# Queries times the per-head matrices: per pair with a block-diagonal matrix, or per head in 64-row tiles

## The chip, the cores and the metric

One NeuronCore of a Trainium2 chip runs the whole program in one launch. The metric is the device time of that launch in microseconds (us); lower is better. TensorE does matmuls (PE in the profile, its weight loads PEld), VectorE is DVE, ScalarE is ACT, SyncE (SP) issues the DMAs. PSUM, where matmuls write, has eight banks of 512 fp32 columns on 128 partitions.

## What is computed

Linear attention with a normalisation feeds two gated feed-forward layers one after the other.

```python
# q, k, v: (8 batches, 8 heads, 576 positions, 64)
kv  = einsum('bhsd,bhse->bhde', k, v)        # one 64x64 matrix per head
o   = einsum('bhsd,bhde->bhse', q, kv)       # the step that is changed
rms = sqrt(mean(o * o, axis=-1) + 1e-6)
x   = (o / rms * g_norm)  -> (4608 tokens, 512)
h   = x @ w_in;  x = (h * clip(h + 3, 0, 6) / 6) @ w_out    # layer 1, d_ff 2048
h   = x @ w_in2; y = (h * cos(h)) @ w_out2                  # layer 2, d_ff 2048
```

All inputs are fp32; the weights are held as float64 and decoded on the chip.

## The kernel before, in words

The 4608 tokens are 36 chunks of 128 tokens (`chunk`, L426) and nine token blocks of 512. A batch has 576 positions, so every ninth chunk from chunk 4 on (4, 13, 22, 31) lies across two batches; `parts` (L409) then gives two halves of 64 tokens. Heads go in four pairs (NP = 4).

`kv_pair` (L393) makes the two 64x64 matrices of a head pair in fp32: head 0 is written to PSUM partitions 0 to 63, head 1 to 64 to 127, and each is copied to its diagonal block of `kvbd` (L406), whose other blocks are zero. `chunk` then does, for 128 tokens: four transposes of q into the bank `pq` (L429), ACT's copy of it to `qT` (L440, head 0 of a pair on partitions 0 to 63, head 1 on 64 to 127), a pause of one turn (W1), the products `po` of the four pairs (L449), ACT's Square and Copy of `po` into `sq` and `ot` (L453, L454), the row sums and the reciprocal root (L459 to L467), the scaling (L469), a pause (W2), four transposes into `px` (L475) and ACT's copy into the layer's input (L481). In fp32 one matmul of the program is two weight loads and two matmul records in the trace; a transpose is one of each.

PSUM has eight one-bank buffers: `acc0` to `acc3`, `P`, `R` and two with the tag `t`. `ps_scratch` (L143) gives the attention its banks. In the prologue (chunks 0 to 3) it goes round the list of L871; after L963 every `kv`, `pq`, `po`, `px` and the tiny `pt` and `pb` of the scale computations take one of the two `t` banks, and so does the bank `Q` of each group of the first layer (L822). A third user waits until one of the two is read out.

The steps are generators that yield between operations; `turn` (L126) advances all that are active. `group` (L813) is one step of a layer's first product: seven products of fp16 operands (L835), after each of which two turns and some of the second product's matmuls (`mm2`, L654) are issued. `attention` (L977) starts a kv pair or a chunk every 0.44 groups, with at most two chunks under way. This gives the order of priority. A scheduler writes each engine's instruction list from it ahead of the launch; an instruction whose operands or bank aren't ready by its own reckoning is put behind ready ones. On the chip each engine runs its list in order.

From 0 to about 33 us the prologue runs, to 167 us the first token block in plain fp32 (L1012, L1027), to 687 us the first layer with the attention's other chunks beside it, and then the rest of both layers.

Of the kernel before, what the change touches and what calls it, by code (L numbers as in the profile page):

```python
# [12 lines left out]
AF = mybir.ActivationFunctionType  # L13
# [42 lines left out]
def attention_moe_kernel(  # L56
# [12 lines left out]
    nc = tc.nc  # L69
    B, H, S, D = q.shape  # L70
# [4 lines left out]
    P = 128  # L75
    NP = H // 2
# [38 lines left out]
    kvbd = const.tile([P, 2, NP, P], F32, name="kvbd")  # L115
# [27 lines left out]
    def ps_scratch(name):  # L143
        tag = scratch[turn_of[0] % len(scratch)]
        turn_of[0] += 1
        return ps_m.tile([P, 512], F32, tag=tag, name=name, bufs=2 if tag == "t" else 1)
# [262 lines left out]
    def parts(c):  # L409

        r, res = 0, []
        while r < P:
            b, s = divmod(c * P + r, S)
            n = min(P - r, S - s)
            res.append((b, s, r, n))
            r += n
        return res
# [8 lines left out]
    def chunk(c, qt, dst, after=None, tmp=None):  # L426
        pt = ps_scratch(f"pq{c}")
        for p in range(NP):
            nc.tensor.transpose(  # L429
                out=pt[:, p * P:(p + 1) * P],  # L430
                in_=qt[:, 2 * p:2 * p + 2, :].rearrange("p h d -> p (h d)"), identity=ident,
            )
        if tmp is not None:
            qT, ot, sq = (tmp[:, n] for n in range(3))
            ot, sq = (t.rearrange("p (h d) -> p h d", h=H) for t in (ot, sq))
        else:
            qT = at_p.tile([P, 512], F32, tag="qT", name=f"qT{c}")
            ot = at_p.tile([P, H, D], F32, tag="ot", name=f"ot{c}")
            sq = at_p.tile([P, H, D], F32, tag="sq", name=f"sq{c}")
        nc.scalar.activation(out=qT, in_=pt, func=AF.Copy)  # L440
        if after is not None:
            after()
        yield
        for _ in range(W1):
            yield
        po = ps_scratch(f"po{c}")
        for p in range(NP):
            for b, s, r, n in parts(c):
                nc.tensor.matmul(  # L449
                    out=po[r:r + n, p * P:(p + 1) * P], lhsT=qT[:, p * P + r:p * P + r + n],  # L450
                    rhs=kvbd[:, b % 2, p], start=True, stop=True,
                )
        nc.scalar.activation(out=sq, in_=po.rearrange("p (h d) -> p h d", h=H), func=AF.Square)  # L453
        nc.scalar.activation(out=ot, in_=po.rearrange("p (h d) -> p h d", h=H), func=AF.Copy)  # L454
        yield
        ss = sm_p.tile([P, H], F32, tag="ss", name=f"ss{c}")
        y = sm_p.tile([P, H], F32, tag="y", name=f"y{c}")
        t = sm_p.tile([P, H], F32, tag="t", name=f"t{c}")
        nc.vector.tensor_reduce(out=ss, in_=sq, axis=AX.X, op=ALU.add)  # L459
        nc.vector.tensor_scalar(out=ss, in0=ss, scalar1=1.0 / D, scalar2=1e-6, op0=ALU.mult, op1=ALU.add)  # L460
        yield
        nc.scalar.activation(out=y, in_=ss, func=AF.Abs_reciprocal_sqrt)
        yield
        nc.vector.tensor_tensor(out=t, in0=ss, in1=y, op=ALU.mult)
        nc.vector.tensor_tensor(out=t, in0=t, in1=y, op=ALU.mult)
        nc.vector.tensor_scalar(out=t, in0=t, scalar1=-0.5, scalar2=1.5, op0=ALU.mult, op1=ALU.add)
        nc.vector.tensor_tensor(out=y, in0=y, in1=t, op=ALU.mult)  # L467
        yield
        nc.vector.tensor_tensor(out=sq, in0=ot, in1=y[:, :, None].to_broadcast([P, H, D]), op=ALU.mult)  # L469
        yield  # L470
        for _ in range(W2):
            yield
        px = ps_scratch(f"px{c}")
        for p in range(NP):
            nc.tensor.transpose(  # L475
                out=px[:, p * P:(p + 1) * P],
                in_=sq[:, 2 * p:2 * p + 2, :].rearrange("p h d -> p (h d)"), identity=ident,
            )
        yield
        for kk, d in dst:  # L480
            nc.scalar.activation(  # L481
                out=d, in_=px[:, kk * P:(kk + d.shape[1]) * P].rearrange("p (k t) -> p k t", t=P),
                func=AF.Copy, scale=gs,
            )
        yield
# [458 lines left out]
    for p in range(NP):  # L944
        run(kv_pair(0, p, kv_t.pop((0, p)), tail))
    run(g_scale())
    isx = tiny("isx", scale["g"][1], imm=8.0)
    pro = [
        chunk(
            c, q_t.pop(c), [(2 * n, xr0[n][:, :, c * P:(c + 1) * P]) for n in range(2)],  # L950
            tmp=wi_p.tile([P, 3, 512], F32, tag="wi", name=f"tmp{c}") if c < 2 else None,
# [3 lines left out]
    n = 0  # L955
# [11 lines left out]
    def run_chunk(c, xr, after):  # L967
        j, n = divmod(c, 4)
        yield from chunk(c, q_t.pop(c), [(0, xr[:, :, n * P:(n + 1) * P])], after)
        free["at"] += 1  # L970
        x_done[j] = x_done.get(j, 0) + 1
        if x_done[j] == 4:
            xraw[0, j] = xr
# [121 lines left out]
    n = NG * (NSB - 2)  # L1095
# [36 lines left out]
```

## Time and profile before

| what | value |
|---|---|
| time, median of 3 runs | 1551.84 us (1547.57 to 1552.95) |
| time of the profiled execution | 1551.0 us |
| its span, first to last instruction | 1549.1 us |
| PE busy | 1516.1 us, 98% |
| DVE busy | 1226.3 us, 79% |
| ACT busy | 1052.3 us, 68% |
| mean granted TensorE clock | 0.998 |

The busy share is an average over stages. Whether an engine sets the time is read from each stage by itself, and from the chain of waits, which follows the work back from its end. A matmul's record lasts longer than the step from one to the next, because matmuls overlap in the array; what a burst costs is read from the distance of the starts.

### The profile page before, as it was taken

To read this page: it belongs to the slowest core of one execution; us is meant where nothing else is said; L and a number is where in the kernel's file an instruction comes from. 1 tells how busy PE (TensorE), PEld (TensorE's weight loads), DVE (VectorE), ACT (ScalarE), POOL (GpSimd) and SP (SyncE) were. 2 spreads that over 40 slices of the span, in tenths; PEclk is the share of its full clock that TensorE was granted. 3 is DMA by queue.
4 is the path that set the end of the run, shared out by engine and by line. 5 is a ranking of instruction groups with operands and counts; after the bars stand their busy time and mean duration, and the time that the engine had idled before them with its cause. 6 is when DMAs were issued, how large, how long until landed. Compare 5 with 4: busy or idle time off the path is not lost.

```text
span 1549.1 us, 28806 instructions
## 1 busy us (share of the span) xinstructions
PE 1516.1 (98%) x11902; PEld 1153.8 (74%) x11902; DVE 1226.3 (79%) x2234; ACT 1052.3 (68%) x1714; POOL 2.0 (0%) x8
## 2 busy tenths in 40 slices
PE   6999999999999999999999999999999999999998
PEld 6444676666667676766666678888888888888887
DVE  4899877786877687876475799989898989889881
ACT  4567665665666565665455788888888887878771
POOL 0000000000000000000000000000000000000000
PEclk9999999999999999999999999999999999999999
DMA  7653433325243342402031233343342424333434
GB/s 205 202 165 95 123 102 110 103 81 165 69 150 98 88 129 74 150 25 79 1 103 48 96 110 117 129 142 116 139 142 105 157 91 155 117 132 123 147 111 155
DMA packets 112067, 180.12 MB, mean 116 GB/s; under 512 B 51008, under 2 KB 83776, under 8 KB 102720
## 3 DMA queue, kind: packets, MB, share of 16 engines
q1 hardware_dynamic: 111936, 178.28, 34.9%
q8 instruction: 93, 1.52, 0.4%
q14 instruction: 38, 0.31, 0.1%
HBM read 144.70 MB, written 33.55 MB: 115 GB/s over the span
## 4 chain that ended last, share of the span: by engine, by line
PE 51%; DVE 31%; ACT 12%; DMA 3%; issue 2%; SPq 1%; ACTq 0%
PE acc L654 18%; PE P L835 10%; DVE uA L587 5%; PE R L835 5%; DVE uA L592 4%; DVE gs_A L264 4%; DVE gs_S L264 4%; ACT uA L589 3%; PE h L1012 3%; PE Q L835 3%; PE acc L1027 3%; DVE c L851 2%; ACT uA L590 2%; PE po L449 2%; PE P L707 2%
## 5 line engine op out<-in xcount | busy, mean ns | idle before, releaser
L835 PEld LDWEIGHTS <-wi 128*128 128x128 f16 x5712 | 557.3, 98 | 108.7 <-issue 5.1
L654 PE MATMUL acc<-g,wo 128*128 128x512 f16 x1536 | 368.9, 379 | 0.4 <-ACT g L561 0.3
L654 PEld LDWEIGHTS <-wo 128*128 128x128 f16 x1536 | 148.8, 98 | 135.0 <-issue 1.7
L835 PE MATMUL P<-xoB,wi 128*128 128x256 f16 x1536 | 190.3, 273 | 1.6 <-ACT sn L847 1.5
L835 PE MATMUL P<-xoT,wi 128*128 128x256 f16 x1536 | 189.1, 273 | 0.5 <-ACT sn L847 0.2
L707 PEld LDWEIGHTS <-gs_A 128*128 128x128 f16 x1632 | 159.7, 98 | 20.4 <-issue 1.9
L847 ACT ACTIVATE sn<-P 128x512 f32<-128x512 f32 x204 | 119.2, 584 | 63.3 <-PE P L835 62.7
L707 PEld LDWEIGHTS <-gs_S 128*128 128x128 f16 x1392 | 136.1, 98 | 22.0 <-issue 6.2
L589 ACT ACTIVATE uA<-uA,cols 128x512 f32<-128x512 f32 x144 | 103.6, 720 | 62.3 <-DVE uA L587 60.9
L548 ACT ACTIVATE u<-c,cols 128x512 f32<-128x512 f32 x96 | 77.9, 812 | 82.2 <-DVE c L851 62.3
L707 PE MATMUL P<-wo,gs_S 128*128 128x256 f16 x888 | 114.6, 273 | 5.0 <-ACT kv_buf L726 5.0
L563 DVE TENSOR_TENSOR g<-u,g 128x512 f16<-128x512 f32 x128 | 87.5, 687 | 30.1 <-ACT g L561 29.1
L707 PE MATMUL P<-wo,gs_A 128*128 128x256 f16 x840 | 107.2, 273 | 1.6 <-ACT kv_buf L726 1.6
L561 ACT ACTIVATE g<-u 128x512 f16<-128x512 f32 x128 | 80.1, 628 | 37.5 <-DVE u L550 36.9
L550 DVE SCALAR_TENSOR_TENSOR u<-u,cols,c 128x512 f32<-128x512 f32 x96 | 71.9, 749 | 39.7 <-ACT u L548 39.4
L262 ACT ACTIVATE gs_A<-uA,cols 128x512 f16<-128x512 f32 x125 | 88.3, 713 | 16.2 <-DVE uA L592 11.3
L264 DVE SCALAR_TENSOR_TENSOR gs_A<-uA,cols,gs_A 128x512 f16<-128x512 f32 x125 | 92.6, 746 | 7.1 <-ACT gs_A L262 5.1
L585 ACT ACTIVATE uA<-c,cols 128x512 int32<-128x512 f32 x108 | 77.2, 715 | 30.0 <-DVE c L856 21.8
L835 PE MATMUL R<-xoT,wi 128*128 128x256 f16 x768 | 94.7, 273 | 0.0
L835 PE MATMUL Q<-xoB,wi 128*128 128x256 f16 x768 | 94.6, 273 | 0.0
L835 PE MATMUL R<-xoN,wi 128*128 128x256 f16 x768 | 94.5, 273 | 0.0
L592 DVE SCALAR_TENSOR_TENSOR uA<-uA,c 128x512 f32<-128x512 f32 x108 | 74.1, 686 | 23.0 <-ACT uA L590 22.1
(205 smaller groups left out, 2242.4 us busy)
## 6 DMA issues: line engine op xcount, KB each, us to landing
wo<-wod SPq DMA_DIRECT2D x63, 1024.0 KB, 4.9
ri<-in_moe_w_in_dram SPq DMA_DIRECT2D x16, 1024.0 KB, 6.5
ro<-in_moe_w_out_dram SPq DMA_DIRECT2D x16, 1024.0 KB, 5.1
x2d<-o SPq DMA_DIRECT2D x36, 256.0 KB, 2.5
xr<-x2d SPq DMA_DIRECT2D x9, 1024.0 KB, 4.8
out_dram<-o SPq DMA_DIRECT2D x36, 256.0 KB, 4.0
q<-in_q_dram SPq DMA_DIRECT2D x30, 256.0 KB, 2.9
kv_buf<-in_k_dram SPq DMA_DIRECT2D x29, 256.0 KB, 2.9
```

The source lines that it names most:

```text
L262: nc.scalar.activation(out=hi, in_=src, func=AF.Copy, scale=s)
L264: nc.vector.scalar_tensor_tensor(out=lo, in0=src, scalar=s, in1=hi, op0=ALU.mult, op1=ALU.subtract)
L548: nc.scalar.activation(out=u, in_=c, func=AF.Relu, scale=u0[:, gi:gi + 1], bias=b0[:, gi:gi + 1])
L561: nc.scalar.activation(out=gt[:, :, 0, sl], in_=u, func=AF.Copy)
L563: nc.vector.tensor_tensor(out=gt[:, :, 1, sl], in0=u, in1=gt[:, :, 0, sl], op=ALU.subtract)
L587: stt(out=u, in0=ui, scalar=nk, in1=c, op0=ALU.mult, op1=ALU.add)
L589: nc.scalar.activation(out=u, in_=u, func=AF.Sin, scale=hf)
L592: stt(out=u, in0=u, scalar=0.5 * SIG2, in1=c, op0=ALU.subtract, op1=ALU.mult)
L654: nc.tensor.matmul(out=acc[e], lhsT=w[:, a, row, e * P:(e + 1) * P], rhs=g[:, c], start=(n == 0 and i == 0), stop=(n == NF - 1 and i == 2),)
L707: nc.tensor.matmul(out=ps[:, mt], lhsT=g[:, c, pr, mt * P:(mt + 1) * P], rhs=w[:, i, a], start=(first and k == 0), stop=(end and k == 2), ...
L835: nc.tensor.matmul(out=ps[bank][:, pr], lhsT=w[:, a, A_AT[an], kk], rhs=x[:, c, kk], start=(first and pr == 0 and i == 0 and kk == 0), sto ...
L847: nc.scalar.activation(out=sn[n], in_=ps["P"], func=AF.Copy)
```

## The change

The product of the queries with `kvbd` is made for each head by itself: contraction over the 64 partitions of that head (`hr`), 128 tokens (or 64) as weights, and the head's 64x64 block as the moving operand. The even heads of the four pairs go into one bank, the odd heads into another. ACT reads each bank with a Square and a Copy of 256 columns, written to every second head's place of `sq` and `ot`.

```diff
-        po = ps_scratch(f"po{c}")
+        po = [ps_scratch(f"po{h}_{c}")[:, 0:NP * D] for h in range(2)]
         for p in range(NP):
             for b, s, r, n in parts(c):
-                nc.tensor.matmul(
-                    out=po[r:r + n, p * P:(p + 1) * P], lhsT=qT[:, p * P + r:p * P + r + n],
-                    rhs=kvbd[:, b % 2, p], start=True, stop=True,
-                )
-        nc.scalar.activation(out=sq, in_=po.rearrange("p (h d) -> p h d", h=H), func=AF.Square)
-        nc.scalar.activation(out=ot, in_=po.rearrange("p (h d) -> p h d", h=H), func=AF.Copy)
+                for h in range(2):
+                    hr = slice(64 * h, 64 * h + 64)
+                    nc.tensor.matmul(
+                        out=po[h][r:r + n, p * D:(p + 1) * D], lhsT=qT[hr, p * P + r:p * P + r + n],
+                        rhs=kvbd[hr, b % 2, p, hr], start=True, stop=True,
+                    )
+        for h in range(2):
+            src = po[h].rearrange("p (m d) -> p m d", m=NP)
+            nc.scalar.activation(out=sq.rearrange("p (m o) d -> p m o d", o=2)[:, :, h], in_=src, func=AF.Square)
+            nc.scalar.activation(out=ot.rearrange("p (m o) d -> p m o d", o=2)[:, :, h], in_=src, func=AF.Copy)
```

## Rows read from the trace of the kernel before

**Rows 1.** The page: its span and the engines' busy time, share, instructions.
```profile
span 1549.1 us, 28806 instructions
PE 1516.1 (98%) x11902; PEld 1153.8 (74%) x11902; DVE 1226.3 (79%) x2234; ACT 1052.3 (68%) x1714; POOL 2.0 (0%) x8
```

**Rows 2.** Stretches: length, busy us of each engine, granted clock, DMA.
```profile
33.00:167.00 134.00, 131.56 (x515) 67.05 (x514) 115.12 (x240) 86.27 (x129) 0.00 (x0) 0.99 0.49 153
167.00:687.00 520.00, 514.45 (x3934) 357.29 (x3932) 397.18 (x831) 319.71 (x533) 0.00 (x0) 1.00 0.34 105
```

**Rows 3.** The chain of waits, 200 to 240 us: start, length, engine, tile, line.
```profile
209.57 0.89 PE po L449 x8
210.47 1.31 PE R L835 x12
211.78 0.44 PE px L475 x4
```

**Rows 4.** Line L449: duration ns min/median/max, first and last start, forms.
```profile
L449 PE MATMUL po<-kvbd,qT x304: 272/275/377, 20.7 to 670.7; 128*128 128x128 f32 x120, 128*64 128x128 f32 x32
```

**Rows 5.** Timeline at one-row matmuls: start, length, engine, line, operation, shapes, count.
```profile
411.11 0.29 PEld L160 LDWEIGHTS pb_o<-cols,ones_row 1*128 1x128 f32 x2 [0.66 <-DVE cols L155]
```

**Rows 6.** Line L160: its loads.
```profile
L160 PEld LDWEIGHTS pb_o<-cols,ones_row x16: 181/182/184, 57.2 to 685.2; 1*128 1x128 f32 x16
```

**Rows 7.** Timeline around one kv pair, 234.5 to 236.4 us.
```profile
234.68 0.60 PE L835 MATMUL R<-xoT,wi 128*128 128x256 f16 x4
...
235.20 0.66 PEld L401 LDWEIGHTS kv<-kv_buf 128*64 128x64 f32 x20 [0.21 <-issue]
235.21 0.80 PE L401 MATMUL kv<-kv_buf 128*64 128x64 f32 x20
...
235.94 0.82 PE L654 MATMUL acc<-g,wo 128*128 128x512 f16 x3
```

**Rows 8.** Line L401: its loads and matmuls.
```profile
L401 PEld LDWEIGHTS kv<-kv_buf x576: 132/138/232, 4.4 to 611.8; 128*64 128x64 f32 x192
L401 PE MATMUL kv<-kv_buf x576: 222/222/366, 4.4 to 611.9; 128*64 128x64 f32 x192
```

**Rows 9.** Timeline of chunk 13, whose tokens lie in two batches.
```profile
280.35 1.09 PE L449 MATMUL po<-kvbd,qT 128*64 128x128 f32 x16
...
281.38 0.39 PE L835 MATMUL R<-xoT,wi 128*128 128x256 f16 x2
```

**Rows 10.** Timeline, 220.6 to 224.2 us: another chunk's px just ahead of po.
```profile
221.38 1.06 PE L449 MATMUL po<-kvbd,qT 128*128 128x128 f32 x8
...
221.59 0.69 ACT L481 ACTIVATE x<-px,cols 128x512 f32<-128x512 f32 x1 [1.12 <-PE px L475]
...
223.35 0.59 ACT L454 ACTIVATE ot<-po 128x512 f32<-128x512 f32 x1
```

**Rows 11.** Timeline, 301.5 to 305.5 us: the same with ACT busy.
```profile
302.26 1.06 PE L449 MATMUL po<-kvbd,qT 128*128 128x128 f32 x8
...
303.60 0.67 ACT L481 ACTIVATE x<-px,cols 128x512 f32<-128x512 f32 x1
```

**Rows 12.** Timeline, 668.5 to 672.5 us: the last such place.
```profile
669.88 1.06 PE L449 MATMUL po<-kvbd,qT 128*128 128x128 f32 x8
```

**Rows 13.** Timeline of PE in the prologue, 14.5 to 21 us.
```profile
14.95 2.34 PE L449 MATMUL po<-kvbd,tmp 128*128 128x128 f32 x12
17.30 0.27 PE L153 MATMUL pt_g<-ident,cols 128*1 128x128 f32 x1
17.41 0.61 PE L449 MATMUL po<-kvbd,tmp 128*128 128x128 f32 x4
```

**Rows 14.** Lines L453 and L481 on ACT: 512 columns, and 256.
```profile
L453 ACT ACTIVATE sq<-po x34: 577/588/613, 22.4 to 671.3; 128x512 f32<-128x512 f32 x34
L481 ACT ACTIVATE x<-px,cols x32: 668/677/702, 107.5 to 681.9; 128x512 f32<-128x512 f32 x32
L481 ACT ACTIVATE xr<-px,cols x8: 463/470/475, 26.9 to 31.9; 128x256 f32<-128x256 f32 x8
```

## The prediction, made before the changed kernel was run

> **What bounds the kernel now.** I read the busy shares of the page first, then the stretches, then the chain of waits where the changed lines run, and last the timeline around them. The page gives PE 1516.1 of 1549.1 us [rows 1]; the stretches show that this is no average over idle and full parts: PE is busy for 131.6 of 134 us while the first token block runs and for 514.5 of 520 us while the other chunks of the attention do [rows 2]. In the second stretch ACT is busy for 319.7 us and DVE for 397.2. The chain of waits there is PE alone, one burst behind the other, `po` among them [rows 3]. So between 33 and 687 us a microsecond more or less on PE, a wait of PE included, is a microsecond of the program, up to the 8 us that PE idles there; ACT and DVE have room.
>
> **What `po` costs now.** L449's records start between 15 and 670.7 us [rows 4, 13], all but the prologue's inside those stretches. A whole chunk's eight take 0.89 us [rows 3], 0.111 a record. Beside it, 12 matmuls of 256 fp16 columns take 1.31 us, 0.109 each. What sets 0.111: the loads or the moving columns? One-row matmuls tell. Two loads of 128 fp32 columns from a single row take 0.29 us together [rows 5], and one lasts 0.182 [rows 6], so the second starts 0.109 us after the first, though only one column moves behind it (matmul form 1x1). A load of 128 fp32 columns thus has a pitch of about 0.11 us, whatever its rows. In the kv pair, with 64-column loads, 20 loads take 0.66 us and one lasts 0.138 [rows 7, 8]: as pairs, nine steps in 0.52 us, 0.058 each, half of 0.11. The pitch goes with the columns loaded, and two column tiles load side by side. So `po` is bound by its loads, and the change doesn't make them narrower: a whole chunk still loads 128 token columns each time, and twice as often.
>
> **The matmuls of a whole chunk (32 of 36).** Eight records become sixteen, in two tiles of 64 rows. No row of this trace has two row tiles, so the price lies between two ends. If they load side by side as the column tiles do, there are eight steps of 0.111, 0.89 us as before; less than that the one-row loads exclude. If the loads take turns, there are sixteen, 1.78 us. I take the first end, because the kv pair is the nearest row: two small tiles alternating in the same way.
>
> The Trainium skill, page "TensorE: Matmul & The Clock Gate", section on packing small matmuls, says that a weight load overlaps running matmuls only where the row group differs. That speaks for the first end, as heads alternate between row groups; no run here has shown it yet, and the sum doesn't use it.
>
> To this comes the change of tile shape, at both ends of the burst. Before the kv pair, the four matmuls of R start at 234.68 and 0.109 apart, the last at 235.01, and the first of kv at 235.21: 0.20 where 0.109 is usual [rows 3, 7]. Behind it the last kv matmul starts at 235.21 + 0.80 − 0.22 = 235.79 and the next burst at 235.94: 0.15 where 0.058 is usual [rows 7, 8]. So 0.09 each. Since the drained array can't load ahead, the first step also takes two loads instead of one, 0.10 more, but the last step counts 0.15 instead of 0.11 + 0.09. The new burst is 0.095 + 0.21 + 6 × 0.111 + 0.15 + 0.01 (the next load, not ahead either) = 1.13 us against 0.89: +0.24. With loads in turn it is 0.095 + 0.21 + 14 × 0.111 + 0.16 = 2.02: +1.13. The first: 32 × 0.24 = **+7.8 us**; the second: 32 × 1.13 = +36.
>
> **The four divided chunks.** They run in two column tiles already: from 280.35 to the next burst at 281.38 is 1.03 us [rows 9], plus the 0.10 ahead that the kv pair shows. The changed form has four tiles of 64x64, with 64 columns loaded and 64 moved. If all four run side by side it is eight steps at the pitch of the kv pair: 0.095 + 0.11 + 6 × 0.058 + 0.16 = 0.71 against 1.13, −0.42; if the row tiles take turns it is 0.46 more, +0.05. Four chunks: **−1.7 us** (to +0.2).
>
> **The second bank.** `po` now holds both `t` banks. Where the bank user before it is its own `pq`, nothing new is waited for: `po` needs the copy of `pq` anyway. But at nine places another chunk's `px` comes directly ahead of `po`; they begin at 221.38 and 302.26, and the last is at 669.88 [rows 10 to 12]. There the odd heads can start only when ACT has copied `px`: at 222.28, 0.90 us after `po` started, or with ACT behind at 304.27, 2.01 us after [rows 10, 11]. Queued behind a waiting matmul on PE is everything, L835 and L654 first. One thing softens it: PE's list isn't in strict program order. In the prologue twelve records of `po` are followed by `pt_g` and then by four more [rows 13], so an unready matmul lets ready ones pass. Then the even heads go alone, eight records at 0.111, and the odd ones alone later, another eight: 0.89 us more than the pairs, and a second change of shape. So a place costs 0.9 to 2.0 us beyond the +0.24; or nothing, if the list puts all of `po` later behind other work. I take 1.1, near the shorter wait, since the longer one needs a late ACT: 9 × 1.1 = **+10 us** (0 to 18).
>
> **The user after `po`** has to wait for the first of the two banks, and the one after that for the second. In the 220 us stretch `po` is free 2.56 us after its first matmul (223.35 + 0.59 − 221.38) [rows 10], and in another place the next user comes 2.2 us after (209.57 to 211.78) [rows 3]. There is little room; I put **+1 us** on it in all (0 to 5).
>
> **ACT.** Two activations of 512 columns become four of 256. Half the columns save 677 − 470 = 207 ns at L481, so one takes about 588 − 207 = 381 ns [rows 14]: 4 × 381 − 2 × 588 = +0.35 us a chunk, 12 us in all, beside 200 idle us of ACT in the long stretch [rows 2]. The row sums now wait for the third activation instead of the first, 0.7 us later; the pauses before `px` hide that. On the path only in the prologue: four chunks, **+1 us** with the slower loads there. Without cover, in full, it would be 12 us.
>
> **The sum.** +7.8 − 1.7 + 10 + 1 + 1 = +18 us on the profiled execution's own 1551.0 us (span 1549.1 and 1.9 around it): 1569. Its time is 0.8 below the median of the runs, which is nothing beside the terms.
>
> **The rivals.**
> *The bank waits cost nothing,* because other ready matmuls fill them and both heads' matmuls stay together: +7.8 − 1.7 + 1 = +7, 1558. For it speaks the passing in the prologue [rows 13], against it that the even heads are ready and will go first.
> *The heads don't run side by side:* row tiles load in turn, so the change doesn't do what it says. +36 + 0.2 + 1, and about 5 for the waits, some of which fall into the longer burst: 1593. For it: no row shows two row tiles. Against it: the column tiles of the kv pair load side by side [rows 7, 8], and each row tile has its own partitions.
> *Faster, on the other side:* the loads of half the rows don't bind, and the steps go at the pitch of the kv pair, 0.058. Then a whole chunk takes 0.095 + 0.11 + 6 × 0.058 + 0.16 = 0.71 us, −0.18, and with the bank waits filled the sum is 32 × −0.18 − 1.7 + 1 = −6.5: 1544. It decides from a load pitch under about 0.08 us for 64 rows by 128 columns. The one-row loads at 0.109 speak against it. The Trainium skill, page "TensorEngine Tiling (Array Packing)", section "Theoretical Speedup", has up to twice the speed for a contraction of 64 or less. That is this rival's direction; the one-row loads of this trace disagree with it for a burst bound by loads.
>
> **How the numbers follow.** The forecast, 1569, has 0.52; waits filled, 1558, 0.20; heads in turn, 1593, 0.17; faster, 1544, 0.07; 0.04 for a schedule that shifts otherwise. A measurement of this kernel can tell about 0.3% (4.7 us) from no change. Faster takes the last rival and a bit, 0.08; same takes a third of the waits-filled case and the low edge of the forecast, 0.13; slower is 0.79. The range goes from 1552 (waits filled, and no cost behind `po`) to 1597 (heads in turn), leaving out the gain and the highest of the heads in turn.
>
> **What would show it.** Right: in the chain of waits the whole chunks' `po` have sixteen records in pairs a few ns apart, at 0.11 a pair and 0.9 to 1.2 us a burst; L449's loads still last about 0.19 us; nine places show the odd heads late or alone; ACT's idle time absorbs four short activations. Wrong: a pair pitch of 0.06 (gain), single records at 0.11 (heads in turn), or PE busy for 514 us of the long stretch with no gaps and no halves (waits filled).

## The result, and the profile after

The changed kernel takes 1567.13 us (median; 1566.28 to 1567.6) against 1550.63 for the kernel before beside it: a ratio of 1.0112, interval 1.0097 to 1.0126. The forecast was 1569, slower. The profiled execution's span goes from 1549.1 to 1565.4 us, +16.3.

The page of after, first the lines that answer [rows 1]:

```profile
span 1565.4 us, 29525 instructions
PE 1536.4 (98%) x12222; PEld 1165.1 (74%) x12222; DVE 1227.8 (78%) x2234; ACT 1058.3 (68%) x1786; POOL 2.0 (0%) x8
```

PE is busy for 20.3 us more in a span that is 16.3 longer; DVE for 1.5, ACT for 6.0. So time went into work on PE and not into waits, but a busy PE isn't a precise measure, since records overlap. The chain of waits of after, 220 to 240 us (start, length, engine, tile, line), shows the work:

```profile
223.02 0.44 PE px L479 x4
223.46 1.03 PE po L451 x8
224.49 0.54 PE acc L658 x2
225.03 1.03 PE po L451 x8
226.06 0.32 PE acc L658
...
233.32 1.31 PE P L839 x12
234.63 1.04 PE po L451 x16
235.67 1.40 PE acc L658 x6
```

Where [rows 3] have one burst of 8 in 0.89 us, there is either one of 16 in 1.04, or, right behind another chunk's `px`, two of 8 with other work between them, 1.03 each. The timeline of after around both (start, length, engine, line, operation, shapes, count, idle time before and what ended it), which answers [rows 10]:

```profile
222.86 0.60 PE L479 MATMUL px<-ident,sq 128*128 128x128 f32 x4
...
223.39 1.10 PE L451 MATMUL po<-kvbd,qT 64*128 64x64 f32 x8
223.50 0.69 ACT L485 ACTIVATE x<-px,cols 128x512 f32<-128x512 f32 x1 [1.12 <-PE px L479]
...
224.42 0.60 PE L658 MATMUL acc<-g,wo 128*128 128x512 f16 x2
...
224.53 0.38 ACT L457 ACTIVATE sq<-po 128x256 f32<-128x256 f32 x1 [0.34 <-PE po L451]
...
224.96 1.10 PE L451 MATMUL po<-kvbd,qT 64*128 64x64 f32 x8
```
```profile
234.03 0.60 PE L839 MATMUL P<-xoT,wi 128*128 128x256 f16 x4
...
234.56 1.11 PE L451 MATMUL po<-kvbd,qT 64*128 64x64 f32 x16
...
235.60 0.82 PE L658 MATMUL acc<-g,wo 128*128 128x512 f16 x3
```

In the second fence the last L839 starts at 234.03 + 0.60 − 0.27 = 234.36, 0.20 before `po`; a usual step is 0.109. Inside, the trace has the 16 records as eight pairs 6 to 7 ns apart, a pair each 0.112 us, but 0.16 from the first pair to the second. From where a plain next record would start (234.47) to L658 at 235.60 is 1.13 us, against 0.89 before. In the first fence both halves have eight single records 0.112 apart, and each takes 1.13 by the same reading, 2.26 in all. The loads last as long as before, and a divided chunk, which answers [rows 9], is shorter:

```profile
L451 PEld LDWEIGHTS po<-kvbd,qT x608: 129/188/330, 22.7 to 687.2; 64*128 64x128 f32 x120, 64*64 64x64 f32 x32
```
```profile
282.50 0.69 PE L451 MATMUL po<-kvbd,qT 64*64 64x64 f32 x32
...
283.13 1.05 PE L839 MATMUL R<-xoT,wi 128*128 128x256 f16 x8
```

0.63 us from the first record to the next burst and 0.09 ahead, 0.72 against 1.12: its 32 records go four at a time, 0.058 apart.

**Where the 16.3 us lie.** The first products of the first layer's groups and of the second layer's mark three stretches. These are rows by line (duration min/median/max in ns, first and last start), of before and then of after:

```profile
L835 PE MATMUL P<-xoB,wi x1536: 269/273/283, 162.3 to 1501.9; 128*128 128x256 f16 x192
L707 PE MATMUL P<-wo,gs_A x840: 269/273/273, 915.2 to 1539.5; 128*128 128x256 f16 x168
```
```profile
L839 PE MATMUL P<-xoB,wi x1536: 269/273/283, 163.9 to 1518.2; 128*128 128x256 f16 x192
L711 PE MATMUL P<-wo,gs_A x840: 269/273/273, 931.5 to 1555.8; 128*128 128x256 f16 x168
```

Up to the first group: 163.9 − 162.3 = +1.6. The middle, which holds the attention's chunks 9 to 35: (931.5 − 163.9) − (915.2 − 162.3) = +14.7. The end: 1565.4 − 931.5 = 633.9 against 633.9, nothing. The middle adds up from its bursts: 13 whole chunks with their heads together at +0.24, nine apart at 2.26 − 0.89 = +1.36, two partly apart with +0.9 in all, three divided at −0.40: 3.2 + 12.3 + 0.9 − 1.2 = +15.1.

### The profile page after: what moved, and what is told of

Read it like the earlier page. It is cut to its first block, busy times and chain, and to the rows that moved or that the text cites. A ratio compares the mean times of both kernels' runs of the same rounds, so it can differ in the third digit from the quotient of the medians.

```text
span 1565.4 us, 29525 instructions
## 1 busy us (share of the span) xinstructions
PE 1536.4 (98%) x12222; PEld 1165.1 (74%) x12222; DVE 1227.8 (78%) x2234; ACT 1058.3 (68%) x1786; POOL 2.0 (0%) x8
## 4 chain that ended last, share of the span: by engine, by line
PE 48%; DVE 34%; ACT 13%; issue 2%; DMA 2%; SPq 1%; DVEq 0%; ACTq 0%
PE acc L658 17%; PE P L839 9%; DVE uA L591 5%; DVE uA L596 5%; PE R L839 4%; DVE gs_A L264 4%; DVE gs_S L264 4%; ACT uA L593 3%; PE h L1016 3%; PE po L451 3%; PE acc L1031 3%; DVE c L855 2%; PE Q L839 2%; ACT uA L594 2%; PE P L711 2%
## 5 line engine op out<-in xcount | busy, mean ns | idle before, releaser
L839 PEld LDWEIGHTS <-wi 128*128 128x128 f16 x5712 | 555.9, 98 | 109.1 <-issue 4.6
L658 PE MATMUL acc<-g,wo 128*128 128x512 f16 x1536 | 369.7, 379 | 1.4 <-ACT o L671 1.1
L658 PEld LDWEIGHTS <-wo 128*128 128x128 f16 x1536 | 147.8, 98 | 136.0 <-issue 2.5
L839 PE MATMUL P<-xoB,wi 128*128 128x256 f16 x1536 | 190.5, 273 | 1.6 <-ACT sn L851 1.5
L839 PE MATMUL P<-xoT,wi 128*128 128x256 f16 x1536 | 189.7, 273 | 0.5 <-ACT sn L851 0.2
L839 PE MATMUL R<-xoN,wi 128*128 128x256 f16 x768 | 94.7, 273 | 0.0
L839 PE MATMUL R<-xoT,wi 128*128 128x256 f16 x768 | 94.7, 273 | 0.0
L839 PE MATMUL Q<-xoB,wi 128*128 128x256 f16 x768 | 94.6, 273 | 0.0
```

The costliest lines, as they stand in the source:

```text
L658: nc.tensor.matmul(out=acc[e], lhsT=w[:, a, row, e * P:(e + 1) * P], rhs=g[:, c], start=(n == 0 and i == 0), stop=(n == NF - 1 and i == 2),)
L839: nc.tensor.matmul(out=ps[bank][:, pr], lhsT=w[:, a, A_AT[an], kk], rhs=x[:, c, kk], start=(first and pr == 0 and i == 0 and kk == 0), sto ...
```

## The experiments

The theory: the whole chunks' `po` is bound by loading 128 columns, so row tiles gain nothing and cost a change of shape at each end of a burst; and the second bank parts the heads at nine places, where the pairs are lost. One table for all. The middle is read for each kernel from the first group product to the 2751st, behind the attention's last chunk (162 to 867 us in before); "po" is the sum of its bursts there, each from the record ahead to the record behind less the usual step of the former, "rest" is the remainder; both come from one profiled execution of each kernel. The stretch up to the first group product isn't in them; it takes 158 to 167 us, 162.3 in before, so the times needn't move as the middles do. A ratio is to the kernel before as it ran beside that kernel (medians 1549.63 to 1550.63).

| kernel | time, us | ratio to before, interval | po, us | rest, us |
|---|---|---|---|---|
| before | 1550.63 | 1 | 25.7 | 679.2 |
| after | 1567.13 | 1.0112 (1.0097 to 1.0126) | 40.5 | 678.9 |
| e2_heads_in_turn | 1579.08 | 1.0187 (1.0172 to 1.0203) | 48.0 | 677.8 |
| e8_two_banks_full_rows | 1575.55 | 1.0172 (1.0155 to 1.0188) | 46.6 | 677.4 |
| e4_quads | 1553.51 | 1.0027 (1.0017 to 1.0036) | 27.3 | 683.9 |
| e5_after_pauses | 1562.89 | 1.0089 (1.0070 to 1.0107) | 34.1 | 678.7 |
| e6_before_pauses | 1552.70 | 1.0013 (1.0001 to 1.0025) | 25.0 | 681.2 |
| e10_two_banks_alone | 1552.59 | 1.0014 (1.0002 to 1.0026) | 29.2 | 682.0 |
| e1_act_alone | 1548.39 | 0.9988 (0.9978 to 0.9997) | 25.7 | 678.5 |
| e3_divided_only | 1549.55 | 0.9994 (0.9985 to 1.0003) | 24.5 | 679.9 |
| e7_quads_pauses | 1557.51 | 1.0038 (1.0024 to 1.0052) | 23.2 | 690.3 |
| e11_quads_22 | 1562.56 | 1.0076 (1.0062 to 1.0091) | 25.1 | 695.0 |
| e9_mixed | 1549.96 | 1.0003 (0.9992 to 1.0014) | 21.9 | 683.2 |

### Do the loads bind, or the rows?

**e8_two_banks_full_rows**: two banks as in the change, but a head's matmul contracts over all 128 rows, so there are no row tiles. The zero blocks of `kvbd` make the result the same.

```diff
-  out=po[h][...], lhsT=qT[hr, p * P + r:p * P + r + n],
-  rhs=kvbd[hr, b % 2, p, hr], start=True, stop=True,
+  out=po[h][...], lhsT=qT[:, p * P + r:p * P + r + n],
+  rhs=kvbd[:, b % 2, p, hr], start=True, stop=True,
```

> The changed kernel with full rows: each head's product contracts over all 128 partitions with that head's 64 columns of the block-diagonal matrix (the other head's rows are zero), in the same two banks, read by the same four activations. No change of tile shape and no row tiles. Theory (the pitch is that of the load, 128 columns, and not of the 64 moving columns): sixteen records at 0.111 us, 1.78 instead of 0.89 of the kernel before; 28 chunks after 33 us give +25, the prologue some 3: about 1579 us. Rival (the moving columns set the pitch): sixteen at 0.056, 0.89 a chunk: about 1551 to 1555 us, the banks' waits alone.

Measured: 1575.55. Its chain of waits at 213 us:

```profile
213.50 1.73 PE po L451 x16
215.23 1.31 PE R L839 x12
```

16 records of 64 moving columns take 0.108 each; eight of 128 moving columns take 0.111 each in [rows 3]. So at 128 loaded columns it makes no difference whether 128 or 64 columns move, and twice the loads are twice the time. Moving columns can set the pitch too, which the prediction left out: before's divided chunks load 64 columns and move 128, and their eight pairs stand 0.109 apart in the trace (1.09 us in all, [rows 9]), where four tiles that load 64 and move 64 take 0.058 in after. These rows fit a pitch that goes with the larger of the two. Row tiles give 1.04 where this gives 1.73: they do run side by side, but that only wins back what cutting the pair into heads had cost.

**e4_quads**: the same four-tile form for whole chunks as the divided ones have, with 64 tokens a matmul.

```diff
-            for b, s, r, n in parts(c):
+            for b, r, n in [(b, r + m, 64) for b, s, r, n in parts(c) for m in range(0, n, 64)]:
```

> The changed kernel with every chunk done as it does the four divided ones: two halves of 64 tokens, so tiles of 64 rows by 64 columns, four at a time, twice as many matmuls. Theory (a load's pitch goes with its columns, and four tiles load side by side): a paired chunk costs 0.72 instead of 1.14 us (17 chunks, -7), a chunk whose heads are apart 1.44 instead of 2.26 (9 chunks, -7), the rest -2: about 1551 us. Rival (an instruction has its price whatever its size, so a step of four costs what a step of two does): eight steps as now, 1567 us.

Measured: 1553.51, 13.6 us below after. A burst takes 0.72 us as in the divided chunks, though it has 32 records where after has 16. The table has `po` at 27.3 against 40.5 in the middle. After, too, moves 64 columns a matmul but loads 128, so this is the plainest proof that the columns of a load were the cost of the change. But the rest grew by 5.0, and the bursts' gain over before, 0.17 a chunk, isn't there in the time. That is taken up below.

**e2_heads_in_turn**: the loop over the heads is outermost, so that the list holds eight records of one row tile and then eight of the other.

```diff
-        for p in range(NP):
-            for b, s, r, n in parts(c):
-                for h in range(2):
+        for h in range(2):
+            for p in range(NP):
+                for b, s, r, n in parts(c):
```

> The changed kernel, with the loop over the two heads outermost: four pairs of the even heads, then four of the odd heads, so that no two row tiles stand next to each other in PE's list. Theory (a 128-column fp32 load has a pitch of 0.11 us per row tile, and the two row tiles load side by side only as neighbours in the list): a whole chunk that is paired now costs 0.095 + 0.16 + 14 x 0.111 + 0.2 = 2.0 instead of 1.14 us; 17 paired chunks after 33 us give +15, the divided ones +2, the prologue some 3: about 1587 us, single records 0.11 apart. Rival (what costs is the change of tile shape and the second bank, and the two row tiles run side by side whatever the order): no change, 1567 us.

Measured: 1579.08, between the two. The chain:

```profile
213.84 1.53 PE po L451 x16
...
226.64 1.03 PE po L451 x8
227.67 0.54 PE acc L658 x2
228.21 1.03 PE po L451 x8
```

1.53, neither 1.04 nor the 2.0 of the theory. In the trace the 16 records of the first burst go as four singles 0.112 apart, then eight with a second row of starts between them, then four singles again. The record that signals the end of the first bank starts at 214.60, the last one at 215.10: two sequences of eight, the second 0.50 us behind the first. So PE had begun the second head, at 214.27, when three records of the first were still to start (214.38, 214.49 and 214.60). That each row tile costs 0.112 a record by itself and that the order of the list decides the overlap is confirmed; that they would take turns in full is refuted.

The Trainium skill, page "TensorE: Matmul & The Clock Gate", section on packing small matmuls, says that weight loads overlap running matmuls where the row group differs, and that matmuls start in the order of the program. After's pairs, 0.112 each, agree with the first. The starts just told disagree with the second: with two row tiles the second head's first record passed three records of matmuls that stand before it. So it isn't true of PE's starts, as the kernel's description has it, that each engine runs its list in order; within each head the starts are in order.

### The places where the heads are parted

**e5_after_pauses** and **e6_before_pauses**: one more turn of pause on both sides of the products (W1 = 2, W2 = 3), in after and, as a control, in before. In e5 only two places have their heads fully apart.

```diff
-W1 = 1
-W2 = 2
+W1 = 2
+W2 = 3
```

> The changed kernel with one more turn of pause ahead of po and ahead of px (W1 = 2, W2 = 3). PE's list then has two chunks whose heads are apart instead of nine. Theory (apart costs 2.26 where together costs 1.14 us): 7 x 1.12 = 8 us less, about 1559 us. Rival (the nine places cost nothing of their own, since other matmuls fill the wait; the loss is the same in every chunk): 1567 us.

> Control: the kernel before with the longer pauses alone (W1 = 2, W2 = 3). Theory (its po has one bank and its chunks' order hides the pauses): within 2 us of the kernel before, 1548 to 1552 us. Rival (the pauses help by themselves, so that the gain of the runs with pauses isn't that of the heads staying together): 1543 us or less.

Measured: 1562.89 and 1552.70. The first lies between its theory and its rival, the second 0.7 us above its range and far from its rival. `po` falls by 6.4 us in the middle, from 40.5 to 34.1, and the rest stays: seven places that closed are 7.9 at 1.13 each, and 1.4 of it come back because five other chunks of e5, two of after, have their heads partly apart. The chain of e5 where after had two halves:

```profile
227.28 1.04 PE po L451 x16
```

So the parting costs what after's fences say. The time fell by 4.2, about half of the 8 expected; the pauses by themselves raise before by about 2 (e6).

**e10_two_banks_alone**: the records of before, unchanged, with pairs 0 and 1 in one bank and 2 and 3 in the other, read by four activations. No row tiles, no more loads.

```diff
-        po = ps_scratch(f"po{c}")
+        po = [ps_scratch(f"po{h}_{c}")[:, 0:2 * P] for h in range(2)]
...
-                    out=po[r:r + n, p * P:(p + 1) * P], ...
+                    out=po[p // 2][r:r + n, p % 2 * P:(p % 2 + 1) * P], ...
```

> The second bank and the four activations alone: the kernel before's eight records of 128 rows with the block-diagonal matrix, the pairs 0 and 1 into one bank and 2 and 3 into the other. In PE's list the two halves stand apart at the same nine places. Theory (what the second bank costs is that halves apart lose their side-by-side running, 1.12 us a place; records that never run side by side lose nothing): 1549 to 1553 us. Rival (the waits for the second bank and of the next user cost of themselves): 1556 us or more.

Measured: 1552.59, about 2 us over before. This lies in the expected range partly by luck: in the profiled executions e10 reaches the first group 3.9 us ahead of before (158.4 against 162.3), 2.3 of it by an accident of before's execution (told below, under the start), and its middle is 6.3 us longer. The halves are parted here too, with nothing lost in pairs:

```profile
218.11 0.45 PE po L449 x4
...
218.99 0.61 PE po L449 x4
```

`po` grows by 3.5 us, 0.4 for each of the nine places, where after pays 1.13 beyond a chunk whose heads are together. A second control lies in e8, which has after's two banks and activations but no row tiles: parted by the same `px`, its two halves take 1.68 here, no longer than its whole burst of 1.73 (1.68 to 1.96 at its nine places).

```profile
226.47 0.84 PE po L451 x8
227.31 0.43 PE acc L658 x2
227.74 0.84 PE po L451 x8
```

Of the second bank's +10 in the change the larger part therefore isn't the bank but the lost overlap and the second change of shape. But the bank isn't free either. The rest of e10's middle grows by 2.8; in it is also a stretch from 268.5 to 272.5 us with a mean granted clock of 0.57, behind a wait of 1.88 us for DVE's `cols` (L155). Before has such a wait too, 1.8 us in this part, and keeps its clock.

### ACT, and the divided chunks

**e1_act_alone**: before with its one bank, read by the four short activations of the change. **e3_divided_only**: the changed form for the four divided chunks alone.

```diff
-        nc.scalar.activation(out=sq, in_=po.rearrange("p (h d) -> p h d", h=H), func=AF.Square)
-        nc.scalar.activation(out=ot, in_=po.rearrange("p (h d) -> p h d", h=H), func=AF.Copy)
+        for h in range(2):
+            src = po.rearrange("p (m o d) -> p m o d", m=NP, o=2)[:, :, h]
+            nc.scalar.activation(out=sq.rearrange("p (m o) d -> p m o d", o=2)[:, :, h], in_=src, func=AF.Square)
+            nc.scalar.activation(out=ot.rearrange("p (m o) d -> p m o d", o=2)[:, :, h], in_=src, func=AF.Copy)
```
```diff
+        if len(parts(c)) == 2:
...          (as in the change)
+        else:
...          (as in the kernel before)
```

> The kernel before with ACT's part of the change alone: po in one bank as before, read by two Squares and two Copies of 256 columns, every second head each. Theory (ACT has room, 0.35 us more a chunk is hidden): within 2 us of the kernel before, 1548 to 1552 us. Rival (ACT's 12 us come out on PE as later banks): 1555 us or more.

> The per-head 64-row tiles in the four divided chunks alone; the other 32 as in the kernel before. Theory (a divided chunk's burst goes from 1.12 to 0.72 us): 4 x 0.40 = 1.6 us less, 1548 us; in the trace, bursts of 32 records in 0.72 us. Rival (the four together don't pay for the second bank and the two more activations): 1550 us or more.

Measured: 1548.39 and 1549.55. The four activations cost nothing; the interval even ends below 1. For e3 the burst is as foretold,

```profile
277.36 0.62 PE po L452 x32
```

against 1.02 in the chain of before,

```profile
280.42 1.02 PE po L449 x16
```

and the time's interval, 0.9985 to 1.0003, holds both the expected −1.6 us and nothing.

### Why shorter bursts don't become a faster kernel

e4's form should beat before by its bursts. Three tries to bring that out:

**e7_quads_pauses** is e4 with W1 = 2 and W2 = 3, **e11_quads_22** is e4 with W1 = 2, and **e9_mixed** uses e4's form only in the 22 chunks from 4 on whose heads it keeps together, and before's form elsewhere.

```diff
-W1 = 1
+W1 = 2
-W2 = 2
+W2 = 3          (e7 only)
```
```diff
+        if c >= 4 and c not in (11, 15, 17, 20, 26, 28, 29, 30, 33, 35):
...          (as in e4_quads)
+        else:
...          (as in the kernel before)
```

> The 64x64 tiles for every chunk (as in the run with quads) together with the longer pauses (W1 = 2, W2 = 3), which leave two chunks whose heads are apart. Theory (a burst of four tiles costs 0.72 us where the block-diagonal one costs 0.89, and what the quads lost again was the nine places at 1.43 to 1.73 us): 26 chunks save 0.17 (-4.4), the four divided ones 0.40 (-1.6), two apart add 1.4, the prologue 0 to -3: 1542 to 1546 us, faster than both kernels. Rival (the second bank costs time wherever po stands, through the next user's wait, and pauses only move it): 1550 to 1553 us.

> Quads with another order: W1 = 2, W2 = 2, three chunks apart. The run with quads and W1 = 2, W2 = 3 lost 11 us outside po in the long stretch against the kernel before. Theory (those 11 us belong to that one list of instructions, which places work ahead of its operands): 1545 to 1552 us. Rival (they come from two banks held by po and will be there in any order): 1555 us or more.

> 64x64 tiles in two banks where the heads stay together, the kernel before's form elsewhere: chunks from 4 on but 11, 15, 17, 20, 26, 28, 29, 30, 33 and 35 (those whose heads stand apart in the changed kernel) as in the run with quads, the rest with the block-diagonal matrix in one bank. PE's list has no chunk apart. Theory (0.72 instead of 0.89 us a burst where the heads are together): 18 x 0.17 + 4 x 0.40 = 4.7 us less than before, 1544 to 1547 us. Rival (as in the run with quads and pauses, what PE saves comes back as waits for ACT and DVE): 1549 us or more.

Measured: 1557.51, 1562.56 and 1549.96; the first expectation was missed by 11 us and more, and its rival's range by 4.5; the other two ended where their rivals had put them. That e11's loss would be there in any order, as its rival has it, isn't shown: with e4's order the rest grew by 4.7 over before. The bursts did what they should, `po` 23.2, 25.1 and 21.9 us against 25.7, but the rest rose by 11.1, 15.8 and 4.0. The waits of PE, 167 to 700 us (who waited for whom, us in all, times, longest), of after, e4, e9 and e11 in turn:

```profile
PE px L479 <- ACT ot L458: 0.6, 2, 0.4
```
```profile
PE px L479 <- ACT ot L458: 2.0, 3, 1.1
```
```profile
PE px L490 <- ACT ot L459: 2.0, 3, 1.1
```
```profile
PE px L479 <- ACT ot L458: 10.0, 7, 2.4
PE po L451 <- DVE kvbd L406: 2.4, 3, 1.4
```

The next user of the banks, `px`, waits for ACT to read `po`. One such place in e11, on the timeline:

```profile
315.34 0.81 ACT L552 ACTIVATE u<-c,cols 128x512 f32<-128x512 f32 x1 [1.36 <-DVE c L855]
316.06 0.36 ACT L457 ACTIVATE sq<-po 128x256 f32<-128x256 f32 x1
...
316.32 0.37 ACT L458 ACTIVATE ot<-po 128x256 f32<-128x256 f32 x1
...
316.75 0.66 PE L479 MATMUL px<-ident,sq 128*128 128x128 f32 x4 [2.27 <-ACT ot L458]
```

The products start at 312.48 and L658 follows them at 313.11. ACT's list has `u` ahead of the reads of `po`, `u` waits for DVE, and PE stands for 2.27 us. Another wait of that kind in e11, 2.4 us up to 389.1, is followed by PE at half its clock (columns: stretch, length, busy us of the engines, granted clock, DMA):

```profile
388.00:394.00 6.00, 4.88 (x20) 2.58 (x21) 3.56 (x9) 3.40 (x9) 0.00 (x0) 0.72 0.00 0
```

That wait cost a second time, the one at 316.75 didn't; in after the longest of the kind is 0.4. In e7 the same mechanism takes only a part of the 11 us: 2.2 us are waits of `px` for `po`'s readers, 5.5 are for the small `pb` matmuls of L160 (3.2 in before), 1.8 for the second product's bank `acc`, and a wait of 1.67 for one `pb` at 480.9 is followed by a mean clock of 0.57 from 482 to 486 us. The pauses alone raise the rest by 2.0 (e6) and the quads alone by 4.7 (e4), so 4.4 of e7's 11.1 arise only with both; how they come about stays open. No kernel of these is faster than before by as much as 0.2%; e1, 0.9988, comes nearest.

## Why the prediction was right, step by step

Forecast +18 on the profiled execution, measured +16.3. By stretches the sum has +2.5 up to the first group (eight whole chunks, one divided, and +1 for the prologue) and +15.5 in the middle; measured are +1.6 and +14.7.

- **Loads bind** [rows 5 to 8]: right for this change. 0.112 a pair in after, and e8 shows 0.108 a record at half the moving columns. That the pitch goes with the loaded columns alone was too narrow: before moves 128 columns as well as it loads 128, and the pairs of its divided chunks show that 128 moving columns take 0.109 by themselves.
- **Whole chunks**, +0.24 each, 7.7 for 32 (the sum has 7.8), with row tiles side by side: +0.24 measured, from the shape change at both ends and the first step. Two parts of the sum were off and cancel: the first step is 0.16 instead of 0.21, and the next burst starts 0.20 behind the last record instead of 0.15 to 0.16.
- **Divided chunks**, −0.42: −0.40.
- **Nine places**, +1.1 each beyond the +0.24: 2.26 − 1.13 = 1.13, nine in number as read from the order of before. The mechanism was the one named (even heads alone, odd heads alone, a second change of shape: 0.89 + 0.24 = 1.13), but the 1.1 had been taken from the wait for ACT, 0.9 to 2.0, and that this comes to the same is luck. PE doesn't stand idle in that wait: at 224.42 two matmuls of L658 fill the time. Not foreseen: two more chunks, at 200 and 564 us, whose heads are partly apart, +0.4 beyond the pairs' price in all.
- **The user after `po`**, +1: 0.6 us in waits of `px`. Right here; e11 shows that this small term is the one that can grow most, to 10 us.
- **ACT**, four activations of about 381 ns: medians 384 and 378, which answer [rows 14]. ACT's busy time rose by 6 us instead of the 12 that the durations add up to, since records on ACT overlap. It costs nothing (e1), as said.
- **The start**, +2.5 by the sum and with it +1 for the prologue: +1.6, the nearness by luck. After's prologue is slower than forecast; its first `h` product (L1016) starts at 30.94, before's (L1012) at 27.96. But before then stands for 2.25 us for DVE's `di` (L254) until 46.9 us and has a mean clock of 0.66 from 46 to 51 us, where after stands for 1.2 and keeps its clock. e3 has before's matmuls in the same order up to 94 us; it stands for 1.7 at this place, keeps its clock, and gains 2.3 us on before there (0.5 ahead of it and 2.8 behind it). With e3's passage in place of before's, the start of after would be +3.9: the prologue's +1 was too small. The stretches of before, e3 and after (length, busy us of PE, PEld, DVE, ACT, POOL, granted clock, DMA):

```profile
46.00:51.00 5.00, 4.12 (x6) 1.84 (x7) 5.00 (x10) 2.47 (x5) 0.00 (x0) 0.66 0.38 114
```
```profile
46.00:51.00 5.00, 5.00 (x31) 2.26 (x30) 4.99 (x11) 3.26 (x6) 0.00 (x0) 1.00 0.56 193
```
```profile
46.00:51.00 5.00, 3.79 (x9) 1.44 (x8) 4.11 (x6) 2.80 (x3) 0.00 (x0) 1.00 0.66 257
```

The two rivals with 1558 and 1593 fall to the same fences: the heads are apart, against "waits filled", and the pairs are 6 ns apart, against "heads in turn". The faster rival, 1544, needed a load pitch below 0.08 us; its reasoning holds for tiles that load and move 64 columns (0.058 in e4), which the change has in four chunks of 36 only. The Trainium skill, page "TensorEngine Tiling (Array Packing)", section "Theoretical Speedup", has up to twice the speed for a contraction of 64 or less; here, against a block-diagonal operand that already filled the rows, whole chunks went from 0.89 to 1.13 us.

## What to carry to other kernels

Before cutting a matmul into smaller tiles, ask what sets the pitch of its records: a one-row or narrow matmul elsewhere in the trace tells loads from moving columns, and only a tile that narrows the binding side, or both sides where they are equal, can gain. Concurrent tiles need their records beside each other in the list for full overlap; a second bank that comes free later parts them, and then the cut costs its full price. And a burst shortened on a full engine is worth nothing until it is seen what the next user of its bank waits for.

## What was not expected of the hardware

- With two row tiles PE began the second tile's records while three of the first, earlier in the list, were still to start (e2: 1.53 us, where the heads apart are two bursts of 1.03).
- The prologue ran its pairs at 0.213 us in after, twice the 0.112 of later. After's profile prints a clock of 1.00 there, but its clock record begins only at 33.8 us; e5, whose bursts from 18.2 to 27 us have the same steps, has a granted clock of 0.50, the lower level of 1.2 GHz, over 17 us:

```profile
16.60:33.70 17.10, 14.58 (x79) 12.77 (x80) 12.00 (x38) 10.24 (x30) 0.00 (x0) 0.50 0.50 143
```

  Before has only 26.8 to 30.2 us of this stretch at the lower level. So after's prologue probably ran at half clock as well, unrecorded, and the steps tell it where the clock column doesn't. The clock may also be why the start was slower than forecast; no run here separates the two.
